# A softplus MLP behind state attention on one core: another written-out order of steps, with other engines for copies, sums and subtractions

## The chip, the core and the metric

The kernel runs on one NeuronCore of a Trainium2 chip. The metric is the device time of one execution in microseconds (us). Three runs of the kernel before gave 615.49, 616.08 and 616.19 us; the median is 616.08 us.

## What is computed

```python
def _attn_ref(x, state):                 # x (8,8,512,64), state (8,8,32,64)
    scores = scale * x @ state^T         # 512 x 32 for each batch and head
    a = softmax(scores)
    xread = a @ state
    scores2 = scale * state @ x^T
    a2 = softmax(scores2)
    sread = a2 @ x
    return concatenate([xread, sread], axis=2)

def _moe_ref(x, w_in, w_out):            # 4352 rows of 512; w_in 512x2048, w_out 2048x512
    h = x @ w_in
    g = np.maximum(h, 0.0) + np.log1p(np.exp(-np.abs(h)))   # softplus
    return g @ w_out
```

The attention's output, heads side by side, goes through the MLP. Both weight matrices arrive as 64-bit words and are put together to 32-bit floats on the core.

## The kernel before, in words

All work is cut into some sixty kinds of steps, each a Python generator with a one-letter name (the table `steps` at the end of the kernel). A string, `PLAN` (lines 40 to 57), holds 1726 letters; the kernel walks through it and runs the next step of the letter's kind. A second table, `ENG` (lines 58 to 83), tells for each run of some kinds which engine does it: A is ScalarE (ACT), D is VectorE (DVE), P is GpSimd (POOL). Every instruction is pinned to program order, so on each engine, and on the DMA queue of SyncE (SP), work is done in the order of the string. Buffers come from pools that are handed out in that order too, first freed first: 8 PSUM banks, 12 small and 17 medium SBUF buffers, and 8 large ones of 1 MB. A step whose buffer is not yet free waits, and what is behind it on its engine or queue waits with it. All instructions are issued through one helper, so the profile puts them on line 99 (L99); they are told apart by operation, tile and time.

A step is named here by its letter and a number that counts from 0: U0 is the first run of U. The kinds that matter:

- Loads on SP: `T` x transposed (batch b, half i is T number 2b + i, 512 KB), `S` state, `I` w_in in pieces (the first four 512 KB, then 1 MB), `O` w_out (eight blocks of 1 MB), `X` x (512 KB), `J` one slab of second-layer weights, 1 MB, read back from DRAM (`slabs`). `j`, `K` write the slabs, `p`, `P` the output.
- Weights: `a`, `A` take the upper bits (ACT), `b`, `B` the lower, `c`, `C` join them (DVE); `D` is a copy rounded to the matmul's type, `E` the remainder; `U`, `W`, `Y` are sums of w_out, their rounded copies and remainders.
- Attention: `Q` scores (PE); `1` transposes them, `2` takes the maximum, `3` subtracts it, `4` the exponential, `5` the sum and its reciprocal, `6` multiplies, `7` transposes back; `8`, `9` are rounded copy and remainder. `e`, `f`, `i`, `t`, `u`, `R`, `r`, `y`, `z`, `Z` are the state's side: `f` its exponential, `t` a transpose on PE.
- First layer: `v` is state times w_in (PE), `h` and `l` its rounded copy and remainder, `g` the product with the softmax (PE), `s` softplus (ACT). The first four tiles of batch 0 are multiplied in plain f32 (g0 to g7), later ones as three passes of rounded parts.
- Second layer of batch 0: `m`, `n` rounded copy and remainder of g, `G` the product with w_out, two halves a tile (G0, G1 are tile 0).
- Second layer of the other batches: seven products on quarter blocks (a Strassen-like form): `F` sums of blocks, `H` rounded copies, `L` remainders, `M` one product of 16 matmuls with one slab, `k` and `q` the sums of the products, `P` the store.

Where the order bears on the start: G0, the first second-layer product, needs s0, and s0 stands on ACT behind A0, which waits for O0. ACT must load another table whenever it changes between softplus and the other functions (`act`, line 139). J takes one of the eight large buffers, which batch 0's w_out, the softplus tiles and the slabs share.

Of the kernel before, what the change touches and what calls it, by code (L numbers as in the profile page):

```python
# [20 lines left out]
B, H, S, NS, D = 8, 8, 512, 32, 64  # L21
# [16 lines left out]
FORMS = (1, 2, 6, 5, 7, 3, 4)  # L38
SLAB = {5: 0, 6: 1, 7: 2, 4: 3, 1: 4, 2: 5, 3: 6}
PLAN = (  # L40
    "TSTSIITITIQI1IQ2O3e12e34dfbaafb4c565OOIIOc6vttQvahb7huecabfuhhbac78gtvggghe1cbhgguaA8c98BC89gvgshsGhll99DUGssB"
    "Am1EWCDbEn2fAaBmcnCgGggGGGGGgbABasmssDCcnEm3XjIXOOIKjvRGGnDsam4mAhhliAlBnBbcnCrYCbEGGggGgGGgGsaDDs2c3mmssEnjSj"
    "jjjjSjKjjjOjTTjOJvvGhhhll5m4hUnEGGgGgn5llU66WAsmdBmsGQvGnYChDlhnE7l7ei89eGggGGsWmsBA8Y9nmn1CUGgGGgKjjjKjKTKTjj"
    "jDffssmEWnY21U32gGGGtttWsouuuoQvvh1lefUYWhUGgshoggKjKKpjKJJjKXglUelogggssWsfsss4Fh3lYHWYggggKXKgsssssHHF5FLYLL"
    "MgRyMMKKppKJJpJJsFFzHkHLFH2LFLrZHkHH4HMMML5L66LkLkk7i1kHMJXXJJMRvvykr8Fh73q9l2h8H9qlkhh4HlMMJPXJJTJlzZkkk35Lgg"
    "gggsLkssss4vvMMgh5qkhlkHhdhsqLLqlllgMgggggMsssssFq67HkLJJJPJPPPXggggMssssHF8LHsHFM6LF7FHFLLkkHMMJJJPJHHkkqqkLL"
    "q98MMtytvuhzHkkuLHlFFLZLhvRMMJJPJJMMHl9kHkhHLHhkLgMMlkirqkLqLklkkPTJJPPJJPJJXXvQvgse1fhshhlq1ell2qh3qggggsssfs"
    "4ggMgggsH2l53LgMg4ssssssgggssHs5Fk6ki7LFHFFHLFHFLtytMMMMkLH6uzkuLZqkHvvRJJJJPTMMhhLlHH7hlHh8q98FLLllkkrMMJJJTJ"
    "XPLFqHLqkk9HLMMgggMMsHsskkqkkkLkJPPJJPTJJXPvQv1khhql2qlee13ggggssshsHfhf42llLgggMgggsHFqL35sss4ssgggMsssH56F6k"
    "LFHkLFH7MMttyF8HqFLu7L9kuzHkLFMJPJPJJMMMJJPPJPPRvHZkkHFqLiLkHh8vMMkLlrHhHhHqLlLlkkH9LLqMJXPTJPPJJJJMgMggMssshk"  # L50
    "kHkklkkvvQge1hfsgggshsshH2Lll3h1l2leLFgggg4sssfsggggssssgMMM3FHFqsH4F5FqqLH5Lqk6LTPPJJJPMtytMMJJXJHFFHkLiuk7kH"
    "HHHzL6HLqLZkukLMMkFMvvRJJPh8hH7kLqlq9LrqLh8MMMJTJPXJJJPPXJPl9kHkhkkklgMMskklkvQvgghqHl1ehe2sfhfLlh13lqgggssss4"
    "Lq253qlgggMMgggJPPPPJs4sssHssw5LiFk6k6gsgggttyMssHzsFHwFLqHFFLMMFZL7HHHHHuqLk7H8kFLMPJJMMJPJJJL9kqLkukLFMRvvMh"
    "lkHLH8HhhklLq9LklMMkrqxhLlkkqkJPJPPJJPMgMkHwxxwyvvgzhsklshhhqlLlxqlZgMgMggssssggggsssskqkqgggggPPJJJPJPgggwsss"
    "xwwwxxxsswsswgxwxxswggsswxgHLFFxwwHssxwxgxLgsMsHHFLFHLMJHHFFHLFLFLFFLHMJMJFLHLFHLHkHHLFkkMJMHHLLFkkMJHHLLqHHLF"
    "LkqkMMJJPJPHLHLkkqLHMFkkLkHLMkHHqLkJJPPMkkqLkkHPLHMqkkqqkLLqPPqMPMkPqMPkqkPP"
)
ENG = {
    '3': "PPDDDPPDPDDPDDDP",
    '6': "PPDPPPPDDPDDDPDD",  # L60
    '8': "PPDPAPDPDPPDAADPAA",
    '9': "DPDPDDDPPDPDDPDDDP",
    'B': "DAAADDAA",
    'D': "PDPAAADA",
    'E': "DDDPDPPD",
    'F': "DPDDDDDDPDPDPDDPDDPDPDDPDDPDPPDPPDPDPDDDDDDDDDDPPDDDDDDDDDDDDDPD",
    'H': "PAAAAPAAAADPAADAPAAAAAAPADPPAAPDDPPDAAPAADDAPDAADADDPAADAAAPAPAPAAPADAAAPAAAAAAADAAAPAADPAAAAADPAAPPPDAAPPPDAPAP",
    'L': "DDDDDDDDPDPDPPPDDDDPPDDDPDPPPDPDDDPDDPPPPPDDPDDDPDDPDPDDDPDDDPDDDPDDDDDDPDDDDDPPDDDDPDDPDDDDDDDDPDDDPDPDPDPDDPDD",
    'U': "PPDDDPDP",
    'W': "AAADAPAD",  # L70
    'Y': "DDDPPPDD",
    'b': "AAAAADDDDD",
    'h': "AAAADADDDDDDDADAADADDDAADDAAADADAADDAADADAAAADAAAAADADADADADAADDAAAD",
    'k': "AADDDDDDDDDDDDDDAADDDDDDDDDDDDDDAADDDDDDDDDDDDDDAADDDDDDDDDDDDDDDDDDDDDDDDDDDDDDDADDDDDDDDDDDDDDADDDDDDDDDDDDDDDDDDDDDDD",
    'm': "DAADAADAAAPADP",
    'n': "DDDPDDDPPDPDDD",
    'o': "AAAD",
    'q': "PPDPDPDDPDPDDPDPPPDDDDPPPPPPPDDPDDPPDDDDPPDDPDDPDDDDDPDPDDDP",
    'u': "DAADDAADDADADDAD",
    'w': "PPAPDPPDDADAAAAP",  # L80
    'x': "DPPPDDPPPPDDDDDD",
    'z': "DDADAAAA",
}


# [934 lines left out]
```

## Time and profile before

| | |
|---|---|
| median of three runs | 616.08 us |
| the profiled execution | 616.8 us |
| its span, first to last instruction | 614.6 us |
| PE busy | 599.0 us, 97% of the span |
| DVE, ACT, POOL busy | 78%, 48%, 45% |
| moved by DMA | 161.62 MB, mean 263 GB/s |
| granted TensorE clock | 1.00 of full speed throughout |

The profiled execution took 2.2 us beyond its span, and 0.7 us more than the median. All differences below are taken within the profiled execution and then put on the median.

### The profile page before, as it was taken

To read this page: it belongs to the slowest core of one execution; us is meant where nothing else is said; L and a number is where in the kernel's file an instruction comes from. 1 tells how busy PE (TensorE), PEld (TensorE's weight loads), DVE (VectorE), ACT (ScalarE), POOL (GpSimd) and SP (SyncE) were. 2 spreads that over 40 slices of the span, in tenths; PEclk is the share of its full clock that TensorE was granted. 3 is DMA by queue.
4 is the path that set the end of the run, shared out by engine and by line. 5 is a ranking of instruction groups with operands and counts; after the bars stand their busy time and mean duration, and the time that the engine had idled before them with its cause. 6 is when DMAs were issued, how large, how long until landed. Compare 5 with 4: busy or idle time off the path is not lost.

```text
span 614.6 us, 10518 instructions
## 1 busy us (share of the span) xinstructions
PE 599.0 (97%) x4112; PEld 488.4 (79%) x4112; DVE 479.2 (78%) x635; ACT 296.8 (48%) x426; POOL 277.8 (45%) x186
## 2 busy tenths in 40 slices
PE   3999999999999999999999999999999999999997
PEld 1577777887788887888788787888788878998886
DVE  4999998799637896798479966699759683259996
ACT  4898857962525218630293318802677322344100
POOL 2432636516653761767276532672030820350581
PEclk9999999999999999999999999999999999999999
DMA  8999959999647888089916982599726947005772
GB/s 304 409 348 377 365 190 344 352 400 415 272 145 258 309 317 358 1 316 370 352 76 245 356 312 125 191 381 419 292 87 218 362 165 299 1 2 187 282 250 68
DMA packets 50415, 161.62 MB, mean 263 GB/s; under 512 B 4288, under 2 KB 29376, under 8 KB 37824
## 3 DMA queue, kind: packets, MB, share of 16 engines
q1 hardware_dynamic: 50368, 160.97, 70.5%
q8 instruction: 32, 0.52, 0.3%
q14 instruction: 15, 0.12, 0.1%
HBM read 137.36 MB, written 23.59 MB: 262 GB/s over the span
## 4 chain that ended last, share of the span: by engine, by line
PE 96%; ACT 1%; DMA 1%; DVE 1%; issue 0%; SPq 0%; ACTq 0%
PE b L99 96%; DMA d<-in_xt_dram 1%; ACT s L99 1%; DVE v L99 0%; DVE s L99 0%; SPq L99 0%; ACT L99 0%; DVE W L99 0%; ACTq L99 0%
## 5 line engine op out<-in xcount | busy, mean ns | idle before, releaser
L99 PE MATMUL b<-g,d 128*128 128x256 f32 (+1 forms) x1576 | 290.1, 337 | 0.0
L99 PEld LDWEIGHTS b<-g,d 128*128 128x128 f32 x1576 | 246.3, 190 | 36.1 <-issue 1.7
L99 PE MATMUL b<-d,d 128*128 128x512 f32 x744 | 176.5, 392 | 0.0
L99 PEld LDWEIGHTS b<-d,d 128*128 128x128 f32 x744 | 138.0, 188 | 33.3 <-issue 4.1
L99 ACT ACTIVATE g<-b 128x512 f32<-128x512 f32 x112 | 64.3, 600 | 89.6 <-PE b L99 84.6
L99 DVE TENSOR_TENSOR s<-s,b 128x512 f32<-128x512 f32 (+1 forms) x105 | 68.9, 676 | 31.1 <-PE b L99 24.9
L99 DVE TENSOR_TENSOR d<-g,d 128x1024 fp32r<-128x1024 f32 x60 | 89.1, 1493 | 4.7 <-ACT d L99 4.6
L99 POOL TENSOR_TENSOR d<-g,d 128x1024 fp32r<-128x1024 f32 x24 | 59.7, 2490 | 45.0 <-ACT d L99 24.7
L99 PE MATMUL b<-g,s 128*128 128x512 f32 (+1 forms) x280 | 71.4, 372 | 0.0
L99 ACT ACT_TABLE_LOAD x48 | 61.6, 1283 | 1.5 <-PEq L1001 0.7
L99 PEld LDWEIGHTS b<-g,s 128*128 128x128 f32 x280 | 50.2, 188 | 12.1 <-issue 1.9
L99 ACT CAST d<-g 128x1024 fp32r<-128x1024 f32 x47 | 48.6, 1050 | 22.9 <-POOL g L99 10.9
L99 DVE TENSOR_TENSOR d<-b,d 128x512 fp32r<-128x512 f32 x62 | 41.6, 682 | 16.4 <-ACT d L99 16.2
L99 POOL TENSOR_TENSOR s<-s 128x256 f32<-128x256 f32 x27 | 27.7, 1028 | 55.6 <-DVE s L99 55.6
L99 POOL TENSOR_SCALAR d<-g 128x1024 fp32r<-128x1024 f32 x22 | 33.0, 1501 | 43.5 <-DVE g L99 28.3
L99 ACT CAST d<-b 128x512 fp32r<-128x512 f32 x33 | 19.0, 585 | 66.8 <-PE b L99 66.8
L99 POOL TENSOR_TENSOR s<-s,v 128x512 f32<-128x512 f32 x15 | 18.9, 1259 | 44.4 <-DVE v L99 43.8
L99 PE MATMUL b<-W,ST 64*32 64x512 f32 (+2 forms) x544 | 32.8, 574 | 4.1 <-DVE W L99 4.1
L99 POOL TENSOR_TENSOR d<-d,d 128x1024 fp32r<-128x1024 f32 (+2 forms) x18 | 29.7, 1648 | 15.3 <-DVE d L99 8.5
L99 DVE TENSOR_REDUCE v<-s 128x16 f32<-128x512 f32 x32 | 21.6, 679 | 16.4 <-ACT s L99 16.3
L99 DVE TENSOR_TENSOR g<-g,g 128x1024 f32<-128x1024 f32 x20 | 27.3, 1364 | 0.4 <-ACT g L99 0.4
L99 DVE TENSOR_TENSOR d<-g 128x1024 f32<-128x1024 f32 x11 | 14.9, 1352 | 13.5 <-ACT g L99 13.5
(83 smaller groups left out, 611.1 us busy)
## 6 DMA issues: line engine op xcount, KB each, us to landing
g<-slabs SPq DMA_DIRECT2D x98, 1024.0 KB, 6.8
d<-in_xt_dram SPq DMA_DIRECT2D x16, 512.0 KB, 6.9
g<-in_w_out_dram SPq DMA_DIRECT2D x8, 1024.0 KB, 13.2
d<-in_xn_dram SPq DMA_DIRECT2D x16, 512.0 KB, 9.2
slabs<-d SPq DMA_DIRECT2D x16, 512.0 KB, 6.9
out_dram<-s SPq DMA_DIRECT2D x56, 128.0 KB, 5.6
g<-in_w_in_dram SPq DMA_DIRECT2D x6, 1024.0 KB, 13.1
slabs<-g SPq DMA_DIRECT2D x24, 256.0 KB, 6.4
```

Of the source, the lines that this page charges most:

```text
L99: return lambda *a, **k: self.tc.keep_in_program_order(f(*a, **k))
```

## The change

The string and the engine table are replaced; nothing else differs. Each kind of step occurs as often as before, and each does the same arithmetic. In the new order the first half batch's softmax runs in one go (Q, 1, Q, 2, 3, 4 with no load between them), with its subtraction on DVE where it was on POOL. The loads of batch 1's transposed x, T2 and T3, stand behind O0 where they were among the w_in pieces ahead of it; Q2, which uses them, stands directly ahead of G0, and t2 behind G8 where it was among the first transposes. From the middle on steps alternate more finely. Over the whole, rounded copies H go from 64 on ACT, 29 on POOL and 19 on DVE to 66, 10 and 36; remainders L from 76 on DVE and 36 on POOL to 71 and 41; the number of changes of ACT's table falls from 48 to 40.

```diff
 PLAN = (
-    "TSTSIITITIQI1IQ2O3e12e34dfbaafb4c565OOIIOc6vttQvahb7huecabfuhhbac78gtvggghe1cbhgguaA8c98BC89gvgshsGhll99DUGssB"
-    "Am1EWCDbEn2fAaBmcnCgGggGGGGGgbABasmssDCcnEm3XjIXOOIKjvRGGnDsam4mAhhliAlBnBbcnCrYCbEGGggGgGGgGsaDDs2c3mmssEnjSj"
-    "jjjjSjKjjjOjTTjOJvvGhhhll5m4hUnEGGgGgn5llU66WAsmdBmsGQvGnYChDlhnE7l7ei89eGggGGsWmsBA8Y9nmn1CUGgGGgKjjjKjKTKTjj"
-    "jDffssmEWnY21U32gGGGtttWsouuuoQvvh1lefUYWhUGgshoggKjKKpjKJJjKXglUelogggssWsfsss4Fh3lYHWYggggKXKgsssssHHF5FLYLL"
...
+    "TSTQ1Q234Ieb1If5a2Itb6accab3IvI4Sevhhhah7f85gbc6cI7dagt8bvOhu8ch9gbgacg9gT9uBAgTsgOCvQsDsheGe8IsXhE9O1IGAllBOm"
+    "jGg21XbfmC2UjaDfAEnB3ggG4bGnGg5cGG34CDIassmsBcmjSIvERnhGj5ltjWOhOsmiGnGlaG67TbiArUgnc6C7Ogu8ma9dgDbEKsOgsWcYsB"
+    "vshnKvGhAlmlhBUGlGnGAgKCgmXsnUDCjjsgE8jghslDBA9GGWsjYgtGEsgYujjmCGgsmjKTgBUmssKnQnvD1EeWYhlGKGfhAjXeGKn2t1UlWG"
+    "mjfWGugYsgs3vKj2vhhJUj3hjlGlKnC4ggKshsGYgW5j4mjllsmGKgTjDijgYHXnnXssgUgEs5jgggssKFLsJTy67M6HjsLFzZM7GGFGHHWFGY"
...
 )
 ENG = {
-    '3': "PPDDDPPDPDDPDDDP",
+    '3': "DPPPPDDDPDPDPPDP",
...
-    'D': "PDPAAADA",
-    'E': "DDDPDPPD",
+    'D': "DDDDAADP",
+    'E': "PDPPDDPP",
...
-    'U': "PPDDDPDP",
+    'U': "DPPDPPPD",
...
-    'n': "DDDPDDDPPDPDDD",
+    'n': "DPDPPDPDPDDPDD",
...
 }
```

## Rows read from the trace of the kernel before

**Rows 1.** The page, first part: busy time, share and instructions of the engines.
```profile
PE 599.0 (97%) x4112; PEld 488.4 (79%) x4112; DVE 479.2 (78%) x635; ACT 296.8 (48%) x426; POOL 277.8 (45%) x186
```
**Rows 2.** The chain that ended last: start us, length us, what.
```profile
18.85 7.71 PE b L99 x60
...
28.52 582.57 PE b L99 x3956
...
611.12 0.42 DVE s L99
```
**Rows 3.** Windows: stretch, busy us of PE, PEld, DVE, ACT, POOL; clock, DMA share, GB/s.
```profile
0.00:28.50 28.50, 16.49 (x156) 9.48 (x156) 19.16 (x36) 17.73 (x32) 8.26 (x16) 1.00 0.94 352
...
125.00:160.00 35.00, 35.00 (x331) 28.95 (x330) 34.83 (x50) 14.99 (x19) 16.35 (x12) 1.00 1.02 411
```
**Rows 4.** Timeline of ACT: A0 with its wait, the softplus table, the next table.
```profile
25.36 1.20 ACT L99 ACTIVATE d<-g 128x1024 f32<-128x1024 f32 x1 [1.84 <-DMA g<-in_w_out_dram]
26.58 1.28 ACT L99 ACT_TABLE_LOAD   x1
27.87 2.07 ACT L99 ACTIVATE s<-b 128x512 f32<-128x512 f32 x4
...
30.99 1.28 ACT L99 ACT_TABLE_LOAD   x1
```
**Rows 5.** Windows of 10 us in the opening, same columns as rows 3.
```profile
10.00:20.00 10.00, 6.71 (x80) 3.64 (x80) 8.93 (x19) 8.88 (x21) 4.25 (x6) 1.00 1.04 404
20.00:30.00 10.00, 9.03 (x56) 6.09 (x49) 9.16 (x14) 8.13 (x12) 3.77 (x5) 1.00 1.02 408
```
**Rows 6.** Timeline of PE: v3; G0 to G1; G4, the first product of tile 2.
```profile
25.41 1.09 PE L99 MATMUL b<-W,ST 64*32 64x512 f32 x16
...
28.52 3.70 PE L99 MATMUL b<-d,s 128*128 128x512 f32 x8 [0.97 <-ACT s L99]
...
39.24 1.03 PE L99 MATMUL b<-g,s 128*128 128x512 f32 x2
```
**Rows 7.** Timeline of PE: three transposes t3 to t5, and what follows.
```profile
99.21 1.47 PE L99 MATMUL b<-ident,s 128*128 128x128 f32 x12
100.61 1.09 PE L99 MATMUL b<-d,ST 64*32 64x512 f32 x16
```
**Rows 8.** Timeline of the opening: POOL's subtraction, the exponential, the first v.
```profile
7.81 1.05 POOL L99 TENSOR_TENSOR s<-s,v 128x512 f32<-128x512 f32 x1 [6.50 <-DVE v L99]
...
8.89 0.63 ACT L99 ACTIVATE s<-s 128x512 f32<-128x512 f32 x1 [6.87 <-POOL s L99]
...
12.89 0.68 PE L99 MATMUL b<-W,ST 64*32 64x128 f32 x16 [4.09 <-DVE W L99]
```
**Rows 9.** Timeline of DVE: C1, D1, b6, E1, n0.
```profile
33.46 1.23 DVE L99 SCALAR_TENSOR_TENSOR d<-d,d 128x1024 int32<-128x1024 int32 x1 [0.30 <-ACT d L99]
34.72 0.69 DVE L99 CAST g<-d 128x1024 fp32r<-128x1024 f32 x1
...
35.93 1.22 DVE L99 TENSOR_TENSOR g<-d,g 128x1024 fp32r<-128x1024 f32 x1
37.07 0.69 DVE L99 TENSOR_TENSOR s<-s,s 128x512 fp32r<-128x512 f32 x1
```
**Rows 10.** Timeline of DVE: the three sums of U3, with POOL idle.
```profile
90.45 0.68 DVE L99 TENSOR_TENSOR d<-d 128x512 f32<-128x512 f32 x1
91.16 0.89 DVE L99 TENSOR_TENSOR d<-d,d 128x256 f32<-128x256 f32 x2
```
**Rows 11.** Timelines of POOL and DVE near the end: two remainders L at once.
```profile
595.35 2.44 POOL L99 TENSOR_TENSOR d<-g,d 128x1024 fp32r<-128x1024 f32 x1
...
595.46 3.42 DVE L99 TENSOR_TENSOR d<-g,d 128x1024 fp32r<-128x1024 f32 x1
```
**Rows 12.** The page, costliest groups: remainders on DVE and on POOL, rounded copies on POOL.
```profile
L99 DVE TENSOR_TENSOR d<-g,d 128x1024 fp32r<-128x1024 f32 x60 | 89.1, 1493 | 4.7 <-ACT d L99 4.6
L99 POOL TENSOR_TENSOR d<-g,d 128x1024 fp32r<-128x1024 f32 x24 | 59.7, 2490 | 45.0 <-ACT d L99 24.7
...
L99 POOL TENSOR_SCALAR d<-g 128x1024 fp32r<-128x1024 f32 x22 | 33.0, 1501 | 43.5 <-DVE g L99 28.3
```
**Rows 13.** Groups by form: remainders in small buffers on POOL, among them those of n.
```profile
L99 POOL TENSOR_TENSOR s<-s,s 128x512 fp32r<-128x512 f32 x6 | 8.7, 1451 | 12.8 <-PE b L99 10.4 <-DVE s L99 2.4
```
**Rows 14.** Tile slabs: issue to landing, alone (555 to 580 us), then at 122 to 142 us.
```profile
DMA to landing us min/median/max: 4.8/4.9/7.2
...
DMA to landing us min/median/max: 7.1/8.8/12.1
```
**Rows 15.** Timeline of PE: 60 matmuls of the products M in one run.
```profile
194.77 10.43 PE L99 MATMUL b<-g,d 128*128 128x256 f32 x60
```

More of the change, by code (lines that the diff above doesn't have):

```diff
@@ L40 @@
 PLAN = (
-    "TSTSIITITIQI1IQ2O3e12e34dfbaafb4c565OOIIOc6vttQvahb7huecabfuhhbac78gtvggghe1cbhgguaA8c98BC89gvgshsGhll99DUGssB"
-    "Am1EWCDbEn2fAaBmcnCgGggGGGGGgbABasmssDCcnEm3XjIXOOIKjvRGGnDsam4mAhhliAlBnBbcnCrYCbEGGggGgGGgGsaDDs2c3mmssEnjSj"
-    "jjjjSjKjjjOjTTjOJvvGhhhll5m4hUnEGGgGgn5llU66WAsmdBmsGQvGnYChDlhnE7l7ei89eGggGGsWmsBA8Y9nmn1CUGgGGgKjjjKjKTKTjj"
-    "jDffssmEWnY21U32gGGGtttWsouuuoQvvh1lefUYWhUGgshoggKjKKpjKJJjKXglUelogggssWsfsss4Fh3lYHWYggggKXKgsssssHHF5FLYLL"
-    "MgRyMMKKppKJJpJJsFFzHkHLFH2LFLrZHkHH4HMMML5L66LkLkk7i1kHMJXXJJMRvvykr8Fh73q9l2h8H9qlkhh4HlMMJPXJJTJlzZkkk35Lgg"
@@ L46 @@
[L46 to L55, printed above, removed]
@@ L56 @@
-    "LkqkMMJJPJPHLHLkkqLHMFkkLkHLMkHHqLkJJPPMkkqLkkHPLHMqkkqqkLLqPPqMPMkPqMPkqkPP"
+    "TSTQ1Q234Ieb1If5a2Itb6accab3IvI4Sevhhhah7f85gbc6cI7dagt8bvOhu8ch9gbgacg9gT9uBAgTsgOCvQsDsheGe8IsXhE9O1IGAllBOm"
+    "jGg21XbfmC2UjaDfAEnB3ggG4bGnGg5cGG34CDIassmsBcmjSIvERnhGj5ltjWOhOsmiGnGlaG67TbiArUgnc6C7Ogu8ma9dgDbEKsOgsWcYsB"
+    "vshnKvGhAlmlhBUGlGnGAgKCgmXsnUDCjjsgE8jghslDBA9GGWsjYgtGEsgYujjmCGgsmjKTgBUmssKnQnvD1EeWYhlGKGfhAjXeGKn2t1UlWG"
+    "mjfWGugYsgs3vKj2vhhJUj3hjlGlKnC4ggKshsGYgW5j4mjllsmGKgTjDijgYHXnnXssgUgEs5jgggssKFLsJTy67M6HjsLFzZM7GGFGHHWFGY"
@@ new lines @@
+    "otoKRoLKrFuRkKJKHokvhQr8hFJlHvH1efLMeJhlMft1pJHL2JLMuiM8Jk9LkqkyPq2lL3tXMMkuF93zkvHXhh4LHhklvJRJlMLgJHlLMh4Fpl"
+    "sHhg5rjZMgHkgssgsg5T6pqsgsgsHksgPJJggLFlssgLgSkksLPHMgq6sgkg7LMTqJskssJsMpJHPJH7FXFdMFHLFLMkMkHFJkLqFJkPLMvHhl"
+    "8hHvHMPLL8kl9kJLJ9JXHqMkMgJqMkhslQkvh1gJsHgh2LhgJFlHJPslgeHMefLJftMuqsg1k233ykHJPssgLztM44uLk5MqqsLkMkZlHigsLg"
+    "skgR5vs6HvJFJkhgqqP6hlqlrggLss7gssggPsHhM8FF9JPykHMsFLFMFHLkLH7LMHzZhJMLJJHLHHMkkJ8HMMkJTLPMPLlPJk9kvFLlkJvhXM"
+    "khllgshMgTXklJsqgvqHQFPskgXhLlk1PehHHegsJ2qgqsgsf1Jk2Ll3Mkfh4sgsHLMFg5glH3PgJsksLgsgLJ45syJgzigssMsPH6gJL7qHsF"
@@ new lines @@
+    "FkLMFTJqFHFHkLkMHPZMMPtJLHJqMuJHtkL8MMLk6qu7vk9JkkhqkvFPhRlHqPTPFMPlhHHLHJMLk89JrLqJMMJlPLgkHqsgMkLLskqgMkgssH"
+    "hkkvlvQJhhkghsJl1gLlse2gfqPhgslgPssgqTlX3sgg41XsggqFgHsJse2Ls5sFgFMs3HFMfMFHLHJJM4LJXkFL5H6tMk7Hk6PMkJLkytqkLq"
+    "MH8JPMvJH7PzLiu98uHkZJHvkhLFJJPRlrLMhMH9JkFLHLMMqkTLlkhgkJshkMHkHMvhPhlklQLJvglq1glsek23MLhlJ12g4qPssfPeMg3gqJ"
+    "ghsw5kP4lsgk5sggsPssgJqsg6FgHsgJgsLsJgMsP6wHs7tFFHLqfM7kFHLFJL8xFtMH9LuuHkMPJkLHJqMMLP8iJkRH9kvkLvrFhMhHlJqlMk"
+    "ghxyJLHLPzJqqHMLFJZsMkhMkJklgsgsglgPvHsLvhkHPlLhlHsMhJgqlqswgsxkhglgPssggggMksPkgwyJJqLzsgxZJggssPwMxkwsxggsqw"
@@ L57 @@
+    "wxxwswgxwwPsxsxkgssxwqwxwqxgHwgxxsPHsFLJsgLsPFHMFLFHFHFLLHFMHFLFMJFLHFHLFkkJHFLMLMHkJkkHHLHJLqJHLFMPqLHLHMHHLk"
+    "JPLLFkHkLLHMHkqMkMkkFJLLJkHqLkPHLkkPqHJHMMHkqLPkLLkkkMqJHPMqLqqkPPPMMqkPqkPP"
 )
 ENG = {
-    '3': "PPDDDPPDPDDPDDDP",
[L60 to L63, printed above, removed]
-    'D': "PDPAAADA",
-    'E': "DDDPDPPD",
-    'F': "DPDDDDDDPDPDPDDPDDPDPDDPDDPDPPDPPDPDPDDDDDDDDDDPPDDDDDDDDDDDDDPD",
-    'H': "PAAAAPAAAADPAADAPAAAAAAPADPPAAPDDPPDAAPAADDAPDAADADDPAADAAAPAPAPAAPADAAAPAAAAAAADAAAPAADPAAAAADPAAPPPDAAPPPDAPAP",
@@ L68 @@
-    'L': "DDDDDDDDPDPDPPPDDDDPPDDDPDPPPDPDDDPDDPPPPPDDPDDDPDDPDPDDDPDDDPDDDPDDDDDDPDDDDDPPDDDDPDDPDDDDDDDDPDDDPDPDPDPDDPDD",
-    'U': "PPDDDPDP",
[L70 to L75, printed above, removed]
-    'n': "DDDPDDDPPDPDDD",
-    'o': "AAAD",
@@ L78 @@
[L78 to L82, printed above, removed]
+    '3': "DPPPPDDDPDPDPPDP",
+    '6': "PPPPDDDPDDDDDPDD",
+    '8': "APAAAAAAAAPADPADDD",
+    '9': "DPDPPDPPPDDDPDPDDP",
+    'B': "DAADDADD",
+    'D': "DDDDAADP",
+    'E': "PDPPDDPP",
+    'F': "DDDDDPDPPDPPDDDDPPDDDDPDPDPDPDDPPDPDDDDPPDPDDDPPDDDDDDDDDDPDDDDD",
+    'H': "AAAAAAAADPDPADAAPDAAPAADADAPAAADADDDAADPPADADAADAAAAAADADADAAPAAAAADDDAADAADADDDDADDADAAPAAADADDADADAAAAPAADDAAA",
@@ new lines @@
+    'L': "DDDDDDPDPDPDPDPDPPDPDDPDDPDDDDPPPDPPPDPDPDPDDDDPDPDPPDPDDDPPDPDPDDPPDDDDDDDPDPDDPDPPDDPDDDDDDDPDDDDPPDDDDDDDPDPD",
+    'U': "DPPDPPPD",
+    'W': "ADAADAAA",
+    'Y': "DDPDDDPP",
+    'b': "AAADDDAADA",
+    'h': "AAAAAADAADAAADAAAAADAADAAAAADDAADAAADDAAAAADADDDDADADAADAAAAADDDDDDA",
+    'k': "ADDDDDDDDDDDDDDDAADDDDDDDDDDDDDDADDDDDDDDDDDDDDDAADDDDDDDDDDDDDDADDDDDDDDDDDDDDDAADDDDDDDDDDDDDDAAADDDDDDDDDDDDDDDDDDDDD",
+    'm': "DAAAADADAPAAAA",
+    'n': "DPDPPDPDPDDPDD",
+    'o': "ADAD",
@@ L83 @@
+    'q': "PDDPDPDDDDPPPDDDPDPDDDPPDPPDPDDPPDPPDPDPPDDPDPPPDDDDDDDPDPDD",
+    'u': "AAAADADADAAAAAAA",
+    'w': "DAADDAPDAAPPAAAA",
+    'x': "PPPPDDPDDDDPDDDD",
+    'z': "AADDADAD",
 }
```

## The prediction

> **What bounds the kernel now.** I read the page first: PE is busy for 599.0 of 614.6 us, no other engine for more than 78% [rows 1]. The chain of waits says the same more sharply. From 28.52 us on it is one piece of PE work, 582.57 us with 3956 matmuls, and after it one DVE addition of 0.42 us and the last store [rows 2]. A new order can't make that piece shorter: it holds the same matmuls, and the granted clock is already 1.00. It can only let it start earlier, or tear holes into it. So two things have to be priced: the 28.5 us ahead, where PE is busy for 16.5 us only [rows 3], and the stalls that the new order may bring behind it, where there were none.
>
> What ends the opening is read from ACT's timeline. A0 starts at 25.36 us after a wait of 1.84 us for the first w_out block, then the softplus table is loaded for 1.28 us, then s0 runs from 27.87 us, and G0 starts at 28.52 us [rows 4, 6]. The DMA sets that: from 10 to 30 us it moves 404 and 408 GB/s with a busy share above 1 [rows 5], so whatever stands ahead of O0 in the queue delays it by its bytes.
>
> **The change, part by part.** The sum is made against the profiled execution (616.8 us, 614.6 us of it the span); the median lies 0.7 us lower, and the difference is put on the median at the end.
>
> *O0 ahead of T2 and T3.* Two loads of 512 KB, 1.05 MB, go behind O0. At 406 GB/s [rows 5] that is 2.6 us: O0 lands at 22.8 us and not at 25.4, and T3, now the last of the same bytes, lands at 25.4. ACT can follow. It waited from 23.5 us on; its first exponential comes 0.4 us earlier, and ahead of A0 b3, b4, f2 and u2 leave it and 80, 82, h4 and u0 come, about 1.5 us less, so it is free near 21.5 us, an estimate from 23.5. A0 (1.20), the table (1.28) and 0.6 for s0 put s0's end at 25.9 us.
>
> *Q2 ahead of G0.* Q2 needs T3, so it starts at 25.4 us and takes 1.1 us (the same number of matmuls of 512 columns as v3's 1.09 [rows 6]). G0 then starts at 26.45 us, 2.07 us earlier than 28.52. This, not s0, is now late last. Were O0 and T3 to come 0.5 us earlier or later, as the engines share the queue unevenly, it moves with them; were T3 hidden, s0 would allow 25.9, so the gain here lies between 1.5 and 2.6 us. PE has the f32 products and v3 done about 1 us ahead of T3; beyond that cover each us of lateness counts in full.
>
> *t2 behind G8.* PE still owes it: three transposes take 1.40 us [rows 7], one 0.47. That leaves 1.6 us.
>
> *The undivided softmax.* The subtraction 30 moves from POOL (1.05 us [rows 8]) to DVE (about 0.7), so the first exponential starts about 0.4 us earlier. I cost this at nothing: the first v waits 4.09 us for joined w_in at 12.89 us [rows 8], long after the softmax's side has its data, and the pieces of w_in come at the DMA's pace. If that cover went, it would be worth at most the 0.4 us.
>
> *The first remainders behind the new start.* G4 needs E1 and n0. Before, n0 ended at 37.76 us and G4 started at 39.24 us [rows 6, 9], 1.5 us to spare. In the new order A1 and B1 stand on ACT behind the softplus of four tiles, one copy of v3 and a table load. With s0 at 25.3 us they end at 31.4, C1 near 32.7; then DVE does 23, U0, D1, E1, n0. U0 was on POOL. With 1.6 us for U0 (the three sums of U3 beside an idle POOL [rows 10]) and the durations of rows 9, n0 ends near 37.4 us. PE reaches G4 10.72 us after G0 [rows 6], at 37.15. So 0.3 us is lost, with bounds of nothing and 1.7 (the contention rival). I take 0.3, from the undisturbed rows, since POOL's only long work there is one remainder.
>
> *Later moves between engines.* Rounded copies H leave POOL (1.50 us each [rows 12]) mostly for DVE, remainders L leave DVE (1.49) for POOL (2.49); eight table loads of 1.28 us go. All of it lies beside PE: I cost it at nothing as long as each engine keeps up. Pricing every step at the mean of its group and adding along the two orders, the largest amount by which an engine's work outruns PE's work in any stretch falls: DVE from about 15 to 11 us, ACT from 10 to 7, POOL from 13 to 7. These are estimates from the groups by form, of which rows 12 and 13 show the costliest kinds. The before order lived with the larger ones without a stall. PE changes between f32 and rounded matmuls for v, R and Q equally often in both, 17 times after the opening, so no time goes there. The end is the same work too: the last matmul, 0.42 us on DVE, the store [rows 2].
>
> *The slab loads.* The largest risk I see in the queue is at J5 to J7. Their large buffers came free three products ahead (8.3 us of PE work; 16 of 60 matmuls in 10.43 us make 2.78 us a product [rows 15]); now they come free two products ahead, 6.0, 6.6 and 6.1 us with the small matmuls in between. A slab that is alone in the queue lands 4.8 us after its issue; at 122 to 142 us, with others ahead, 7.1 us and more [rows 14]. The queue should be nearly empty then, because the new order does about 3 us more PE work before it needs the same bytes; so nothing, between nothing and 4 us.
>
> **Sum.** 2.07 − 0.47 − 0.3 = 1.3 us: 615.5 us on the profiled execution's scale, 614.8 on that of the median. A measurement of this kernel can tell about 0.2% (1.2 us) from no change, so this forecast lies on the edge of it.
>
> **The rivals.**
>
> *Larger lead.* O0 and T3 land 0.5 us earlier and n0 is not late: 2.07 + 0.5 − 0.47 = 2.1 us, up to 2.6 with early stalls of the first products gone as well: 613.5 us. For it speaks that the opening has 12 us of idle PE; against it that the DMA there is full already.
>
> *The lead is used up between DVE and POOL.* At 595.46 us a DVE remainder with two SBUF inputs took 3.42 us, begun 0.11 us after one of POOL's of 2.44 us: POOL's remaining 2.33 and then about 1.1 of its own [rows 11]. If U0, E1 or n0 meets n1 on POOL in this way, n0 is late by another 1.45 us [rows 13], and the lead goes: 2.07 − 0.47 − 1.75 = −0.15, 616.2 us. The Trainium skill, "SBUF — State Buffer", section "Who interferes with whom", has it as a rule that a DVE instruction with two SBUF inputs and a GpSimd instruction that reads SBUF exclude each other for the whole instruction; by that rule, with U0 moved onto DVE beside POOL's work, the time would be 616.2 us. The trace agrees with the rule at 595 us. Against the rival: POOL does not reach n1 before s3's copy is made at 34 us, so only E1 and n0 can meet it, and DVE may well come first. The same collision can happen later, where E4 ends about 0.7 us ahead of the first product of tile 8 by my reckoning.
>
> *Slower: late slabs.* If the queue is as full at J5 as it was at 122 to 142 us, J5, J6 and J7 land 7.1 to 8.2 us after their issue and PE stands for 1.3, 0.7 and 2.1 us, 4 us together: 1.3 − 4 gives 618.8 us. It decides from the point where more than 1.2 us of other transfers are ahead of J5. For it: a DMA busy share of 1.02 between 125 and 160 us [rows 3]. Against it: of the transfers next to J5 only one output store of 256 KB stands ahead of it.
>
> *It does not do what it says.* The strings differ in order alone, and instructions are pinned, so the order will be as written; but T2 and T3 could be harmless where they were if O0 was late for another reason. Then G0 stays near 28.5 and t2 costs its 0.47: 616.5 us.
>
> **How the numbers follow.** I give the forecast 0.42, the larger lead 0.13, the used-up lead 0.22, the late slabs 0.12, no effect at the start 0.06, and 0.05 for stalls that I have not found, at some 617.5 us. The forecast's own range, 614.2 to 615.5 us, lies on both sides of the 0.2% line, so about 0.34 of its 0.42 counts as faster and 0.08 as the same. Faster: 0.34 + 0.13 = 0.47. The same: 0.08 + 0.22 + 0.06 = 0.36. Slower: 0.12 + 0.05 = 0.17. The range goes from 613.2 us (the larger lead with its own uncertainty) to 618.2 us, which leaves out most of the slab case and little else.
>
> **What would show it.** Right: ACT's A0 near 22.8 us with little or no wait, Q2 waiting for T3 until about 25.4, G0 at 26 to 27 us, one PE stall of some tenths ahead of G4, and then one piece of PE work of about 583 us in the chain. Wrong: A0 at 25 us again; a PE wait for DVE of over 1 us near 37 or 70 us; PE waiting for slabs near 140 us; or a PE piece that is broken up later, with DVE as releaser, in the stretch of the products M.

## The result and the profile after

The changed kernel took 623.42 us in the median of four runs (622.66 to 625.68), against 616.13 us for the kernel before beside it. The ratio is 1.0127, with an interval of 1.01 to 1.0154: slower by 1.3%, and above the range of 613.2 to 618.2 us. The profiled execution took 622.66 us, 620.9 of it the span, 6.3 us more than before; the medians lie 7.3 us apart. It is the fastest of the four; the slowest had a mean granted clock of 0.996 where the other three had 0.999.

The page's first part shows more busy time on VectorE and GpSimd, for the same work (before: [rows 1]):

```profile
PE 602.2 (97%) x4112; PEld 488.9 (79%) x4112; DVE 495.0 (80%) x628; ACT 297.5 (48%) x441; POOL 291.8 (47%) x170
```

The chain of waits (start us, length us, what) was one piece of PE work before [rows 2]. Now it is torn: from 38.7 to 64.8 us it runs over POOL, ACT and DVE, and once more over ACT at t4, from 93.8 to 96.2 us:

```profile
15.78 22.89 PE b L99 x118
...
61.44 3.30 DVE W L99
64.78 28.98 PE b L99 x167
...
96.18 63.01 PE b L99 x576
...
159.31 458.08 PE b L99 x3006
```

Behind 160 us nothing is broken. PE's timeline (start us, us, ..., idle time ahead and who ended it) has the places. v4 stands in the rows at 45.61 and 47.72, v5 and v6 in those at 61.34 and 64.78, t4 at 96.18:

```profile
45.61 1.54 PE L99 MATMUL b<-W,ST 64*32 64x512 f32 x8
47.72 1.06 PE L99 MATMUL b<-W,ST 64*32 64x512 f32 x8 [0.56 <-DVE W L99]
...
61.34 1.06 PE L99 MATMUL b<-W,ST 64*32 64x512 f32 x8
64.78 1.92 PE L99 MATMUL b<-W,ST 64*32 64x512 f32 x24 [2.38 <-DVE W L99]
...
96.18 0.63 PE L99 MATMUL b<-ident,s 128*128 128x128 f32 x4 [0.85 <-ACT d L99]
```

Before, v4 with R0 behind it, and v5 with v6, read:

```profile
46.58 1.09 PE L99 MATMUL b<-W,ST 64*32 64x512 f32 x16
47.60 1.10 PE L99 MATMUL b<-d,s 128*32 128x64 f32 x64
...
65.17 1.95 PE L99 MATMUL b<-W,ST 64*32 64x512 f32 x32
```

The idle time understates the stalls, because a matmul that waits in the middle of a step is drawn long: the first eight matmuls of v4 take 1.54 us in the rows of after, where all sixteen took 1.09 before. From one step's start to the next one's, v4 to R0 took 3.10 us where it took 1.02 before, v5 to v6 3.89 instead of 0.89, v6 to the next product 1.40 instead of 0.99, G22 to t4 2.37 where a G alone takes 1.36. That is 2.1, 3.0, 0.4 and 1.0, in sum 6.5 us. G0 started at 27.41 us instead of 28.52, which gives 1.1 back, and t2, now behind G8, costs 0.45. 6.5 + 0.45 − 1.1 is 5.9 of the 6.3 us; the rest is in pieces of under 0.4 us that I did not follow.

v4 multiplies the columns that c7 joins, v5 those of c9. DVE's timeline shows the joins C2, c7, c8, C3 and c9:

```profile
40.95 2.07 DVE L99 SCALAR_TENSOR_TENSOR d<-d,d 128x1024 int32<-128x1024 int32 x1
...
44.26 3.40 DVE L99 SCALAR_TENSOR_TENSOR W<-d,d 128x1024 int32<-128x1024 int32 x1
...
54.80 2.00 DVE L99 SCALAR_TENSOR_TENSOR W<-d,d 128x1024 int32<-128x1024 int32 x1
56.73 2.07 DVE L99 SCALAR_TENSOR_TENSOR d<-d,d 128x1024 int32<-128x1024 int32 x1
...
61.36 3.37 DVE L99 SCALAR_TENSOR_TENSOR W<-d,d 128x1024 int32<-128x1024 int32 x1
```

Before, such a join took 1.23 us [rows 9]. POOL's timeline shows what stood beside each: 33 beside C2, E2 beside c7, n4 beside c8, 63 and then 94 beside C3, E3 beside c9:

```profile
39.90 2.04 POOL L99 TENSOR_TENSOR s<-s,v 128x512 f32<-128x512 f32 x1
43.83 2.75 POOL L99 TENSOR_TENSOR g<-d,g 128x1024 fp32r<-128x1024 f32 x1 [1.89 <-DVE g L99]
...
54.44 1.28 POOL L99 TENSOR_TENSOR s<-s,s 128x512 fp32r<-128x512 f32 x1
55.68 2.03 POOL L99 TENSOR_TENSOR s<-s,v 128x512 f32<-128x512 f32 x1
57.68 2.27 POOL L99 TENSOR_TENSOR d<-s,d 128x512 fp32r<-128x512 f32 x1
60.91 2.73 POOL L99 TENSOR_TENSOR g<-d,g 128x1024 fp32r<-128x1024 f32 x1 [0.97 <-DVE g L99]
```

c7 begins 0.43 us after E2 and ends 1.08 us after E2's end (47.66 against 46.58); c9 likewise ends 1.08 us after E3's (64.72 against 63.64). C2, c8 and C3 end 1.08 to 1.09 us behind the ends of 33, n4 and 63 as well. So a join that comes second waits for all of POOL's instruction and then does nearly all of its own work. It goes the other way too: 33 took 2.04 us on POOL where such a subtraction took 1.05 [rows 8]. The Trainium skill, "SBUF — State Buffer", section "Who interferes with whom", has this as its rule: a DVE instruction with two SBUF inputs and a GpSimd instruction that reads SBUF exclude each other, and the later one waits to the end. These rows agree.

The profile puts t4's wait down to ACT. But on DVE l8 stands behind Y3, and Y3 took 2.44 us beside the remainder E6 on POOL. Without that remainder (experiment 2), and with Y3 put behind l8 (7), t4 doesn't wait. Y3 in DVE's timeline:

```profile
92.99 2.44 DVE L99 TENSOR_TENSOR d<-d,d 128x1024 fp32r<-128x1024 f32 x1
```

The windows from 45 to 66 us (busy us of PE, PEld, DVE, ACT, POOL; clock, DMA share, GB/s), before and then after, show POOL's busy time going from 6 to 15 us while PE loses 3:

```profile
45.00:66.00 21.00, 21.00 (x176) 15.92 (x182) 20.24 (x27) 18.34 (x23) 5.98 (x5) 1.00 1.04 361
```

```profile
45.00:66.00 21.00, 17.94 (x163) 11.37 (x165) 20.86 (x24) 15.69 (x23) 15.25 (x11) 1.00 0.74 289
```

DVE has no room for it. From 28 us to the end of c9 it ran 42 instructions in either kernel. Those of before took 35.7 us; two of them were long beside POOL, by 2.2 us in sum over the shortest time of their form, which leaves 33.5. Those of after took 38.6 us, and the same 42 took 29.2 us in experiment 8, where POOL is nearly empty. So the new order and table gave DVE some 4 us less to do there, and the meetings with POOL took 9.4 us where they had taken 2.2. c9 ended at 64.72 us, before at 62.46:

```profile
61.24 1.22 DVE L99 SCALAR_TENSOR_TENSOR W<-d,d 128x1024 int32<-128x1024 int32 x1
```

And it was due earlier: four products, G12 to G15, stood ahead of v5 before, which began at 65.17; now they come after v6, and v5 begins at 61.34.

### The profile page after: what moved, and what is told of

It is laid out like the page before. It is cut to its first block, busy times and chain, and to the rows that moved or that the text cites. A ratio compares the mean times of both kernels' runs of the same rounds, so it can differ in the third digit from the quotient of the medians.

```text
span 620.9 us, 10499 instructions
## 1 busy us (share of the span) xinstructions
PE 602.2 (97%) x4112; PEld 488.9 (79%) x4112; DVE 495.0 (80%) x628; ACT 297.5 (48%) x441; POOL 291.8 (47%) x170
## 4 chain that ended last, share of the span: by engine, by line
PE 92%; DVE 4%; ACT 1%; issue 1%; DMA 1%; POOL 0%; SPq 0%; ACTq 0%
PE b L99 92%; DVE v L99 1%; DVE s L99 1%; DVE W L99 1%; DVE d L99 1%; DMA ST<-in_zp_dram 1%; ACT s L99 1%; ACT d L99 0%; POOL s L99 0%; ACT L99 0%; SPq L99 0%; DVE g L99 0%; ACTq L99 0%
## 5 line engine op out<-in xcount | busy, mean ns | idle before, releaser
L99 POOL TENSOR_TENSOR d<-g,d 128x1024 fp32r<-128x1024 f32 x32 | 86.6, 2712 | 90.5 <-DVE d L99 56.6
L99 DVE TENSOR_TENSOR d<-g,d 128x1024 fp32r<-128x1024 f32 x52 | 80.6, 1550 | 11.7 <-ACT d L99 11.7
L99 ACT CAST d<-b 128x512 fp32r<-128x512 f32 x38 | 21.7, 586 | 54.1 <-PE b L99 48.7
L99 POOL TENSOR_TENSOR d<-d,d 128x256 f32<-128x256 f32 (+1 forms) x17 | 27.5, 1620 | 42.5 <-ACT d L99 22.0
L99 PE MATMUL b<-W,ST 64*32 64x512 f32 (+2 forms) x544 | 35.7, 579 | 4.9 <-DVE W L99 4.8
L99 POOL TENSOR_TENSOR s<-s,v 128x512 f32<-128x512 f32 x15 | 19.7, 1318 | 41.5 <-DVE v L99 28.5
L99 ACT COPY s<-b 128x512 f32<-128x512 f32 (+2 forms) x33 | 16.8, 536 | 42.0 <-PE b L99 27.0
L99 DVE TENSOR_TENSOR d<-d,d 128x1024 fp32r<-128x1024 f32 (+2 forms) x25 | 30.7, 1229 | 2.7 <-POOL d L99 1.8
L99 POOL TENSOR_TENSOR g<-g,g 128x1024 f32<-128x1024 f32 x11 | 29.2, 2657 | 3.0 <-ACT g L99 2.8
L99 POOL TENSOR_TENSOR d<-g 128x1024 f32<-128x1024 f32 x6 | 15.4, 2571 | 27.0 <-ACT g L99 27.0
```

Source lines behind the costliest of these rows:

```text
L99: return lambda *a, **k: self.tc.keep_in_program_order(f(*a, **k))
```

## The experiments

The theories. **Stretch**: POOL's instructions with two inputs hold up DVE's joins, DVE is full, so PE waits. Against it: **another chain** (n1, 33, 43, a7 feed c7 late); **queue order** (c9 stands behind four steps that are less urgent); and for the opening, **O0's landing** against **PE's own work and clock**.

**1. E2, E3 and E6 on DVE** (`remainders_on_dve`).

```diff
-    'E': "PDPPDDPP",
+    'E': "PDDDDDDP",
```

> The changed kernel with E2, E3 and E6 (remainders of w_out) on DVE and not on POOL. In the changed kernel c7 took 3.40 us beside E2, c9 3.37 us beside E3 and Y3 2.44 us beside E6, where such an operation takes 1.22 us alone, and PE stood for about 2.3 us ahead of and within v4, 3.4 us about v5 and 1.0 us ahead of t4. Theory 1 (DVE's two-input operation stands until POOL's remainder is done): these three stalls shrink to under 1 us together although DVE gets 3.7 us more work; the time falls by 4 to 6 us, to 617.5 to 619.5 us. Theory 2 (the joins are late because too much stands ahead of them on DVE and ACT): the added work makes it worse or leaves it, 623 to 626 us.

Measured: 624.65 us, ratio 1.0128 (1.0113 to 1.0143), no gain. c7 fell to 1.21 us and v4's stall from 2.1 to 0.5. But E3 now stood on DVE itself ahead of c9, which ended at 64.41 us, v5 still waited 2.6 us, and t4 1.5. Stretch is right for c7; what POOL gives up, DVE must do, and so the time is the one that the second theory gave.

**2. The same three steps writing zeros only, on POOL** (`remainders_write_only`).

```diff
-            elementwise(wout[k][:, :, 1], pair(wf[k].t), f32(wout[k][:, :, 0]), ALU.subtract, engine())
+            if k in (2, 3, 6):
+                nc.gpsimd.memset(f32(wout[k][:, :, 1]), 0.0)
+            else:
...
```

> The changed kernel with E2, E3 and E6 left out of the computation: POOL fills the three remainder blocks with zeros in their place, an operation that writes SBUF and reads nothing (the low parts of six of sixteen tiles of w_out are thus zero in batch 0). Theory 1 in its narrow form (it is POOL's reading that shuts DVE's second input out): c7, c9 and Y3 take 1.2 to 1.3 us where no other POOL operation runs beside them, the stalls at v4 and t4 go and v5's shrinks to about 1 us; 617 to 619 us. Theory 2: c7 ends less than 1 us earlier, 622 us or more.

Measured: 620.99 us, ratio 1.0075 (1.0053 to 1.0097), 2.4 us below the changed kernel, between the forecasts of the two theories. c7 and c9 are back at 1.2 us, and the stalls at v4 and t4 fell from 2.1 and 1.0 us to 0.5 and nothing. v5 kept 2.2 us. DVE's timeline has c8, C3, m5 and c9:

```profile
55.24 2.00 DVE L99 SCALAR_TENSOR_TENSOR W<-d,d 128x1024 int32<-128x1024 int32 x1
57.17 2.07 DVE L99 SCALAR_TENSOR_TENSOR d<-d,d 128x1024 int32<-128x1024 int32 x1
...
59.79 1.78 DVE L99 CAST s<-s 128x512 fp32r<-128x512 f32 x1
...
62.69 1.21 DVE L99 SCALAR_TENSOR_TENSOR W<-d,d 128x1024 int32<-128x1024 int32 x1
```

c8 and C3 still met n4 and 63. m5, a plain copy that took 0.39 us in experiment 8, took 1.78 us beside the end of 94 and a write of zeros on POOL from 60.34 to 61.29 us. So part of the lateness comes from steps that were not changed here.

**3. Subtraction 33 on DVE** (`subtraction33_on_dve`).

```diff
-    '3': "DPPPPDDDPDPDPPDP",
+    '3': "DPPDPDDDPDPDPPDP",
```

> The changed kernel with subtraction 33 on DVE and not on POOL. There it waited behind n1, held up 43 on ACT, and a7 behind 43; a7 ended at 43.65 us, c7 began at 44.26 us. Theory 1: C2 takes 1.2 us and not 2.07, but c7 still meets E2; the stall at v4 shrinks by at most 1 us, time 622 to 623.5 us. Theory 2 (the chain n1, 33, 43, a7, c7 makes v4 late): a7 ends 2 to 3 us earlier and the stall at v4 of 2.3 us goes, 620.5 to 621.5 us.

Measured: 624.84 us, ratio 1.013 (1.0112 to 1.0149). C2 took 1.21 us instead of 2.07, and c7 still took 3.40 us beside E2: the stalls stayed 2.0 us at v4 and 3.4 at v5. Counted from G0, a7 ended only 0.3 us earlier, not 2 to 3, so this run alone doesn't decide on the other chain. Experiments 1 and 2 do: they leave the chain over 33 as it was, and v4's stall fell from 2.1 to 0.5 us. The other chain falls.

**4. The new string with the old engine table** (`order_new_engines_old`), and **5. the old string with the new table** (`order_old_engines_new`). Each is the string of one kernel with the table `ENG` of the other.

> The new order with the engine table of before: separates the two tables. Theory 1: with E2 back on DVE, and 32, 33 and n1 too, v4 no longer waits; E3 was already on DVE's side in neither of the collisions but D0 and D2 return to POOL, so others may come: between 616 and 621 us. Theory 2 (the order is at fault, whatever the engines): 622 to 626 us.

> The string of before with the engine table of after: the fourth corner beside before (616.3 us), after (623.4) and the new string with the old table (646.9). Theory A (the table is to blame: it puts more two-input work on GpSimd): slower by 5 us or more, about 622 us. Theory B (the new string's due times are to blame, the table is harmless): 616 to 618 us. Theory C (string and table fit only each other, since each step's buffer and engine were chosen together): far slower, 630 us or more, with stalls all along.

Measured: 646.91 us, ratio 1.0492 (1.0475 to 1.051), and 669.57 us, ratio 1.087 (1.0842 to 1.0899). In both, stalls lie along the whole kernel: between 160 and 600 us PE was busy for 430.0 and 424.3 of 440 us, where before and after have 440.0. Neither theory of the first expectation allowed for that; the third of the second holds. The two parts fit only each other, so "which of them is to blame" has no answer by swapping.

**6. c9 ahead of the steps in front of it** (`join9_earlier`).

```diff
-iArUgnc6C7Ogu8ma9dgDbEKsOgsWcYsBvshn
+iArUgnc6COgu8a9dgbcDEKsOgs7mWYsBvshn
```

> The changed kernel with c9 straight behind C3 on VectorE, and 73, m5, D3, W1 behind it (b9 moved with it on ScalarE); E3 stays on GpSimd. Theory A (the new order puts v5 on TensorE 4 us earlier than before while c9 stands behind four other steps in VectorE's queue): c9 ends near 61.1 us plus what the opening is late, the stall at v5 falls from 3.0 to 0.5 us or less, v6 to G12 grows to about 1 us since D3 and E3 come later, 620.5 to 622 us. Theory B (what GpSimd's remainders do to the joins is all of it): c9 meets the end of 94 or E3 as before, the stall at v5 stays above 2 us, 623 us.

Measured: 624.04 us, ratio 1.0115 (1.0098 to 1.0131), no gain. PE's timeline:

```profile
63.50 1.95 PE L99 MATMUL b<-W,ST 64*32 64x512 f32 x32
65.38 0.50 PE L99 MATMUL b<-g,s 128*128 128x512 f32 x1
66.28 3.23 PE L99 MATMUL b<-g,s 128*128 128x512 f32 x13 [0.41 <-POOL g L99]
70.59 1.67 PE L99 MATMUL b<-g,s 128*128 128x512 f32 x6 [1.08 <-DVE s L99]
```

v5 and v6 run through: queue order does set the place of that stall. It doesn't set the sum. The products behind now wait for E3, n5 and E4, 0.7, 1.4 and 0.7 us by their starts: 2.8 us where v5 and v6 had lost 3.4. So the first theory is right on v5, and its time of 620.5 to 622 us did not come.

**7. Repairs together** (`repaired`): the string of 6, E2 and E3 on DVE, Y3 behind l8.

```diff
-    'E': "PDPPDDPP",
+    'E': "PDDDDDPP",
...
-D1EeWYhlGKG
+D1EeWhlYGKG
```

> The changed kernel with c9 straight behind C3 (as in the run before it), E2 and E3 on VectorE as they were in the kernel before, and Y3 behind l8. If the three stalls were each made where the reading of the trace says, v4 keeps 0.5 us, v5 and t4 nothing, G12 up to 0.5 us: 623.4 less 1.6, 3.0 and 1.0 is 617.8 us, between 617 and 619.5. If VectorE simply has too much to do between 28 and 66 us, the stalls move behind v6 to G12 and G13, and the time stays above 620 us.

In the kernel before, only E2 was on DVE; E3 was on POOL there too, at 49.05 us.

Measured: 622.43 us, ratio 1.0091 (1.0076 to 1.0106). v5 and t4 no longer wait and v4 loses 0.5 us, but PE's timeline shows the next one, G14 held up in its middle by n5, by 1.8 us; G16 loses 0.7 for E4:

```profile
61.17 2.13 PE L99 MATMUL b<-W,ST 64*32 64x512 f32 x32
63.23 3.47 PE L99 MATMUL b<-g,s 128*128 128x512 f32 x14
68.19 2.56 PE L99 MATMUL b<-g,s 128*128 128x512 f32 x10 [1.49 <-DVE s L99]
```

n5 itself took 1.76 us there beside a sum on POOL, where it takes 0.69 alone. Each stall was where the reading put it, and the summing of repairs was wrong: a full engine hands its lateness on to whoever is due next.

**8. GpSimd emptied between 38 and 64 us** (`gpsimd_emptied`).

```diff
+        k = (now[0], count[now[0]] - 1)
+        if k in NONE:
+            return
+        if k in COPY:
+            return nc.scalar.copy(dst, a)
+        if k in FEW:
+            dst, a, b = dst[:, :, 0:4], a[:, :, 0:4], b[:, :, 0:4]
         (nc.vector if e == "D" else nc.gpsimd).tensor_tensor(dst, a, b, op)
...
+    NONE = {("n", 1), ("n", 3), ("n", 4), ("9", 4)}
+    COPY = {("E", 2), ("E", 3)}
+    FEW = {("3", 3), ("6", 2), ("6", 3)}
...
```

> The changed kernel with GpSimd nearly emptied between 38 and 64 us: the remainders n1, n3, n4 and 94 are left out (their products use the rounded copy twice), 33, 62 and 63 work on four columns of 32 only, E2 and E3 are plain copies on ScalarE. The string, the buffers and the number of matmuls stay. Theory A (VectorE's instructions are stretched by what GpSimd does beside them; from 28 us to c9 its 42 instructions took 38.6 us where their forms take 29.7 us undisturbed): c6, C2, c7, c8, C3 and c9 take about 1.22 us each, the stalls at v4 and v5 and ahead of G12 fall from 5.5 us to under 0.6 in sum, the one at t4 stays, so the time is 617 to 618.7 us. Theory B (the order alone makes c7 and c9 late, since four other steps stand ahead of c9): the joins are short, but v5 still waits over 1.5 us, 620 us or more.

Measured: 620.36 us, ratio 1.006 (1.004 to 1.0079). On DVE, c7, c8, C3 and c9:

```profile
44.89 1.22 DVE L99 SCALAR_TENSOR_TENSOR W<-d,d 128x1024 int32<-128x1024 int32 x1
...
54.31 1.23 DVE L99 SCALAR_TENSOR_TENSOR W<-d,d 128x1024 int32<-128x1024 int32 x1 [0.43 <-ACT d L99]
55.45 1.22 DVE L99 SCALAR_TENSOR_TENSOR d<-d,d 128x1024 int32<-128x1024 int32 x1
...
58.96 1.23 DVE L99 SCALAR_TENSOR_TENSOR W<-d,d 128x1024 int32<-128x1024 int32 x1 [0.15 <-ACT d L99]
```

On PE, v4, then v5 with v6:

```profile
47.67 1.09 PE L99 MATMUL b<-W,ST 64*32 64x512 f32 x16
...
61.82 2.55 PE L99 MATMUL b<-W,ST 64*32 64x512 f32 x32 [0.46 <-ACT s L99]
```

No wait of v4 to v6 for DVE is left. String and queue order are those of the changed kernel, so stretch alone is enough for the stalls there, and they don't need c9's place in the queue. v4 loses nothing, v5 0.5 us for ACT, which now has two copies more, the product behind v6 0.5: 1.0 us where it was 5.5. The span fell by 2.6 us only, because in this profile G0 started at 29.64 us, 2.2 later than in the profile of after. That is why the time came out above the 617 to 618.7 expected. By the time alone it would count for the second theory; by the joins and v5, which were the signs to tell them apart, it is the first.

**9. The opening's edit alone, in the kernel before** (`start_edit_alone`). T2 and T3 behind O0, Q2 directly ahead of G0, the steps that need Q2's scores and t2 after it.

```diff
-TSTSIITITIQI1IQ2O3e12e34...vttQvahb7huecabfuhhbac78gtvggghe1cbhgguaA...vgshsGhll99DUGss
+TSTSIIIIQI1IQ2OTT3e12e34...vttvahb7hucabuhhbac78gvggghcbhggaA...vgshsQGhll99DUGefe1ss
...
-...hhliAlBnBbcn...
+...hhliAltuBnBbcn...
```

> The kernel before with the opening's edit alone: T2 and T3 behind O0, Q2 directly ahead of G0, the steps on Q2's scores behind G0, t2 some 20 us later; everything else as before. Theory 1 (the prediction's step: O0's landing sets the opening): G0 starts near 26.5 us, about 2 us earlier, and no new stall of 1 us, so 614 to 615 us. Theory 2 (without Q2 PE is idle more in the opening, and its matmuls run at the clock's lower level for longer, as g0 and g1 do in the profile after, at 2.04 and 1.6 to 1.9 us where they took 1.14 and 1.02): G0 starts at 27.4 to 28.6 us, and the time is 615.2 to 616.5 us.

Measured: 620.02 us, ratio 1.0058 (1.0043 to 1.0073), above what either theory gave. ACT's timeline, with a5 and A0 in the first row, then the softplus table and s0:

```profile
20.47 2.25 ACT L99 ACTIVATE d<-g 128x1024 f32<-128x1024 f32 x2
22.74 1.28 ACT L99 ACT_TABLE_LOAD   x1
24.03 1.08 ACT L99 ACTIVATE s<-b 128x512 f32<-128x512 f32 x2
```

s0 runs 3.8 us earlier than before [rows 4], as the prediction wanted. PE's timeline, with g0, Q2 and G0:

```profile
16.88 2.05 PE L99 MATMUL b<-s,s 128*128 128x256 f32 x4
...
27.24 1.09 PE L99 MATMUL b<-d,ST 64*32 64x512 f32 x16
28.26 3.27 PE L99 MATMUL b<-d,s 128*128 128x512 f32 x7
```

G0 gains 0.26 us, not 2. PE is busy without a gap from g0 to G0, and Q2 is part of that work. The span is 3.5 us longer than before. Counted from step to step, 1.2 us of that stand at G4, where E1 and n0 are late, 0.5 at v4 and 1.3 at G22, all behind G0 and this variant's own; that they come from the steps on Q2's scores, which now fall into DVE's full stretch, is likely but not shown.

**10. Extra matmuls in the opening's idle time** (`warm_start`), and **11. the same on top of 8** (`gpsimd_emptied_warm`).

```diff
+    def warm(n):
+        t = banks.take()
+        for _ in range(n):
+            nc.tensor.matmul(t[:, 0:P], ident, ident, start=True, stop=True)
+        banks.free.appendleft(t.tag)
+    WARM = {("Q", 2): 7, ("t", 1): 4, ("v", 1): 3, ("v", 2): 3}
...
+        if (k, count[k]) in WARM:
+            warm(WARM[k, count[k]])
```

> The changed kernel with 17 extra products of the identity matrix with itself on TensorE, in its idle stretches between 8 and 16 us; their results are not used. Theory A (TensorE's clock is at its lower level in g0 and g1 because the opening gives TensorE too little to do): g0 and g1 take about 1.0 us each, v2 starts near 19.3 us as soon as c3 is there, G0 near 27.2 us in each profile, against 27.4 to 28.8 in the runs so far; the later stalls stay, so 622 to 622.8 us. Theory B (the late G0 of three runs has another source, such as the loads): G0 at 28 us or later again and 623.4 us.

> The run before it, with the 17 extra products of the identity matrix on TensorE between 8 and 16 us. If the clock's lower level in g0 and g1 holds the opening back and VectorE has no backlog that takes the gain, G0 comes near 27.2 us and the time is 1.0 to 1.4 us below the run before it. If the gain is taken by another wait, the times of the two agree within 0.4 us although G0 comes earlier.

PE's timeline of the profile after, g0 with g1, then g2 to g7:

```profile
15.78 3.42 PE L99 MATMUL b<-s,s 128*128 128x256 f32 x8 [0.82 <-DVE s L99]
...
20.16 5.45 PE L99 MATMUL b<-s,s 128*128 128x256 f32 x24
...
26.41 1.06 PE L99 MATMUL b<-d,ST 64*32 64x512 f32 x16
27.41 1.99 PE L99 MATMUL b<-d,s 128*128 128x512 f32 x4
```

Eight matmuls took 3.42 us where a third of the next 24 takes 1.82, 1.9 times as long. That is the clock's lower level, 1.2 GHz, for most of them, although the column of the granted clock reads 1.00 in every window of this stretch. With the extra matmuls the same eight are (PE's timeline of 10):

```profile
17.15 1.97 PE L99 MATMUL b<-s,s 128*128 128x256 f32 x8
```

From the start of Q1, which waits for its load, to G0 it was 19.96 us in 10 and 19.97 in 11; without extra matmuls 20.20 in the profile of after and 21.02, 20.86 and 21.54 in those of 1 to 3. The steps behind g1 tell the same: from start to start t1 and v2 took 0.53 and 0.60 us in the profile of after, 0.99 and 1.04 in that of 8. So the clock was at its lower level where PE had been mostly idle, and how long it stayed there differed between executions. The Trainium skill, "TensorE: Matmul & The Clock Gate", Part 1, says that an idle array is gated to 1.2 GHz and that the number of slow matmuls at the start varies from run to run; these rows agree.

What it is worth depends on what comes behind. With POOL's work in place 10 took 624.35 us (ratio 1.0126, 1.0108 to 1.0144), above both forecasts: nothing gained, and c7 and c9 took 3.41 and 3.37 us as in the profile after. With GpSimd emptied, 11 took 618.79 us (ratio 1.0036, 1.002 to 1.0051), 1.6 us less than 8 on the same chip. In the profiles G0 started at 27.94 us in 10, against 27.41 in that of after, and at 28.33 in 11, against 29.64 in 8. By these two pairs a lead at G0 counts only if DVE can follow.

No kernel of these beats the one before. An estimate says why. The nine steps that 8 takes from POOL or cuts down (n3, 63 and E3 of them were on POOL before too) would cost DVE, done there, 0.7 to 1.2 us each, 7.2 in sum; with the 29.2 us of 8 that is about 36 us, no less than the 35.7 it took before, and c9 is due 3.8 us earlier.

## Why the prediction was wrong

*What bounds the kernel: right.* PE's piece of work was torn, and nothing behind 160 us matters.

*O0 ahead of T2 and T3: right, with more room than predicted.* O0 landed at 21.2 us instead of 22.8, T3 at 23.7 instead of 25.4. A0 ran at 23.22 us without a wait; ACT was not free near 21.5 us, as I had estimated, but 1.7 us later, and s0 still ended near 26.3 us, ahead of Q2's end.

*Q2 ahead of G0: the first step that failed.* "PE has the f32 products and v3 done about 1 us ahead of T3." It had not: Q2 started 2.7 us behind T3's landing, because PE was still at g2 to g7 and v3. Q2's 1.06 us used to lie in PE's idle time of the opening; the change moved it into a stretch without a gap. And I priced g0 and g1 as in the trace of before, although the moved Q2 and t2 were PE work that stood ahead of them there, Q2 ahead of g0 and t2 ahead of g1. The lead was 1.1 us in the profile of after; in the seven other profiles with this opening and no extra matmuls (one of them, 4, with the old engine table) G0 started between 28.45 and 29.65 us, so it was mostly nothing. Experiment 9 shows it on the kernel before.

*t2 behind G8: right* (0.45 us). *The first remainders: right.* G4 to G5 took 1.79 us in both kernels; nothing was lost there, of 0.3 predicted.

*Later moves between engines, costed at nothing: the step that cost the most, 6.5 us.* The estimate of how far each engine's work outruns PE's fell for DVE, from 15 to 11 us. It was made with mean durations of groups, and a mean doesn't know which instruction stands beside which. DVE's undisturbed work to c9 did fall, by some 4 us; its meetings with POOL rose by 7.2. *The slab loads: right*, no product M waits for one.

*The rivals.* "The lead is used up between DVE and POOL" had the mechanism, rows and rule included, and gave it 0.22. I looked for it at U0, E1 and n0 and priced one meeting of 1.45 us, with a floor at 616.2 us. It came at c7 and c9, where PE has no other work left, and cost up to 3 us a time. I even named E4 as a later place and added no price for it. Late slabs did not happen. Of no effect at the start the reason did not come, since O0 did land earlier, but in seven profiles G0 stayed near 28.5 us or later all the same.

*What would show it.* Of the signs written down, the PE wait for DVE of over 1 us came, at 46 and 61 us and not near 37 or 70.

What stays open: how much of the 3.0 us at v5 is owed to its earlier due time. With POOL nearly empty (8) the early v5 waits for no join. No run has the stretch and v5 as late as before, so the two are not taken apart where POOL does its work.

## What to carry to other kernels

Before two engines get more work at the same time, list for each step on the bound's path what stands beside it on the other engine; a table of busy time per engine doesn't show that they exclude each other. A stall behind a full engine moves when it is repaired: repair its load, not its place. And work moved out of an idle stretch was free there: ask what it costs at its new place, and what its absence does to the clock.

## What the runs showed of the hardware beyond that

A stall can halve the clock behind it. In 1, PE was idle for some 2 us ahead of v6, and the windows from 65 us on read:

```profile
65.00:66.00 1.00, 1.00 (x20) 0.17 (x8) 1.00 (x2) 0.42 (x1) 0.38 (x1) 0.72 0.00 0
66.00:67.00 1.00, 1.00 (x8) 0.00 (x0) 1.00 (x2) 0.98 (x3) 1.00 (x1) 0.50 0.52 176
```

A granted clock of 0.50 is the lower level, 1.2 GHz. v6 to the next product took 2.20 us there, 1.40 in the profile of after, where a wait of 2.38 us was followed by a clock of 1.00.
